# Forward attention of a decode block on one Trainium2 core: K and V of heads 32 to 111 loaded by pairs in 2 MB transfers

## The chip, the cores and the metric

The kernel runs on one core of one Trainium2 chip, in one launch. The metric is the device time of that launch in microseconds; for the kernel before the change it is the median of three runs. All data stands in HBM at the start, and all results have to be in HBM at the end.

## What is computed

The program is a decode step of one transformer block (4 sequences, one token each) with its gradients. Cut to what matters here:

```python
# x: (4, 1, 512); k_cache, v_cache: (4, 32, 4096, 128); all bfloat16
q = (layernorm(x) @ wq).reshape(4, 1, 32, 128).transpose(0, 2, 1, 3)
p = softmax(einsum("bhqd,bhkd->bhqk", q, k_cache) * 128 ** -0.5)
o = einsum("bhqk,bhkd->bhqd", p, v_cache)
h = x + o.transpose(0, 2, 1, 3).reshape(4, 1, 4096) @ wo
out = h + (silu(layernorm(h) @ w1) * (layernorm(h) @ w3)) @ w2
# returned: out, and the gradients of x, k_cache, v_cache, wq, wo, w1, w3, w2 for a given grad_out
```

4 sequences times 32 heads make 128 "heads" s, with sequence b = s % 4 and head h = s // 4. Each has 1 MB of K and 1 MB of V. The program reads K once (134 MB), V twice (268 MB) and writes the gradients of both caches (268 MB).

## The kernel before

Everything is written in one fixed order; each engine works through its own instructions in that order and waits on semaphores. There are three stretches.

**Forward** (`for gi in range(NGI)`, L653 to L715): 64 steps `gi`, two heads a step. For the two heads of a step: `T_pe` and `T_dve` transpose K (a quarter on TensorE, copied out by ScalarE in L362; three quarters on VectorE in 32x32 blocks of 32-bit words, L367). `S_head` makes the scores of both heads in one PSUM tile of 128 x 256 with 32 small matmuls (L393), whose stationary parts (`W`, `zq`) GpSimd prepares one step ahead in `q_stationaries` (L373, L375). Softmax is spread over the engines: `sm_max` (VectorE, L400 and L402), `sm_max_T` (TensorE, L407), `sm_gmax` (VectorE, L412), `sm_bcast` (TensorE, L417), `sm_exp` (VectorE copy L422, ScalarE L425), `sm_sum` (TensorE L431), `sm_norm` (VectorE L436, ScalarE L439), `sm_P` (TensorE L446, four ScalarE copies L450 into `P_all`). Then `PK_pairs` (GpSimd, L456) writes P twice beside each other, and `PK_mul` (VectorE, L460) multiplies K by P. `M_mm` (TensorE, L475) sums, over 32 groups of 128 keys, V-transposed times [P*K, P]: 32 matmuls of 128 rows x 128 columns by 130 columns into one PSUM bank. `M_end` adds P*K over the keys with ones as stationary operand (L485) and copies the sum M out (ScalarE, L489). M (kept until the gradients) holds what the gradient of q needs and the output o.

A step does the softmax of its own heads, the transposes of the next step's heads (`na`, `nb`), and `M_mm`/`M_end` of two heads that lie 3 and 2 behind (`m1`, odd; `m2`, even). `M_mm(m1)` is split into 16 and 16 matmuls around `sm_max_T`, `M_mm(m2)` into 24 and 8 around `sm_P`. Every 32 heads `kP_flush` empties the P*K sums; every 16 heads `O_cols` copies columns of o.

**Middle** (L717 to L972): output projection, layer norm, the gated MLP and its gradient; a chain of small steps.

**Backward** (L975 to L1519): V again, gradients of V (L816, L1403 on VectorE) and of K, written out 1 MB at a time for heads 0 to 31 and by pairs of heads (2 MB, 64 keys per partition for each head) for heads 32 to 127; `P_rows` (L1357) builds for these pairs the pair layout of P from `P_all`.

**Buffers and queues.** K, V, transposed K, PK, M and all weights live in `arena`, 23 slots of 1 MB (a little more, for alignment). `Slot` takes the slot that has been free longest; `give` returns it. All large transfers are issued by SyncE in program order and pass through one queue, first in, first out. Each load waits, on SyncE, for the last readers of its slot. `load_K` fills K up to 8 heads ahead (`more_K`, after each `PK_mul`), `load_V` always 3 heads ahead (`VQ`, after each `M_end`). In both, partition p of a head holds keys 32p to 32p+31, so a transfer is 128 rows of 8 KB.

Of the kernel before, what the change touches and what calls it, by code (L numbers as in the profile page):

```python
# [23 lines left out]
OLD = 9  # L24
LEAD = 64


@with_exitstack
def kernel(
# [80 lines left out]
    free = deque(range(NSLOT))  # L110
    part = {"B": False, "side_done": False}
    SIDE = ("Pp", "lnb", "wq2", "dqflat", "fin", "rows1", "rows2", "oflat", "w2a", "w2b", "gwq", "gw2", "gw13", "gwo")
# [13 lines left out]
    class Slot:  # L126
        def __init__(self, name, src=free):
            self.i = src[0]
            if part["B"] and src is free:
                lone = sorted((i for i in free if i not in part["pairs"]), key=age, reverse=True)  # L130
                self.i = lone[0] if name in SIDE or lone and age(lone[0]) >= OLD else max(free, key=age)
            src.remove(self.i)
            self.w = arena[:, self.i * SLOT:(self.i + 1) * SLOT]
            o = (self.i + 1) % 2 * LEAD
            self.t = self.w[:, o:o + SJ * Dh]

        def b(self, n=4096):
            return self.t[:, 0:n]
# [36 lines left out]

    Ks, Vs, KTs, PKs = {}, {}, {}, {}

    def load_K(s):
        if s < NH:
            Ks[s] = Slot("Kn")  # L180
            nc.sync.dma_start(out=Ks[s].heads(), in_=cache_head(A_k_cache, s))

    nvl = {"n": 0}

    def load_V(s):
        if s < NH and s >= nvl["n"]:
            nvl["n"] = s + 1
            Vs[s] = Slot("Vn")
            nc.sync.dma_start(out=Vs[s].heads(), in_=cache_head(A_v_cache, s))


    def more_K(s):
        while len(Ks) + kdone["n"] < min(NH, s + 8) and len(free) > 1:
            load_K(len(Ks) + kdone["n"])

    kdone = {"n": 0}
    more_K(0)


# [11 lines left out]
    for i in range(2):  # L211
# [3 lines left out]
        onesw.append(t)  # L215

    def ones_window(col):
        i = col % 2
        return onesw[i][:, 32 - i - col:64 - i - col]

    rowg = fcon.tile([P, 8], FP32, name="rowg")
    nc.vector.tensor_reduce(out=rowg[:], in_=ident_f.rearrange("p (c g q) -> p g c q", c=4, q=4), axis=AX.XY, op=ALU.add)
    quad = fcon.tile([P, 4], FP32, name="quad")
    nc.vector.tensor_reduce(out=quad[:], in_=ident_f.rearrange("p (q i) -> p q i", q=4), axis=AX.X, op=ALU.add)
    bsum = fcon.tile([P, P], FP32, name="bsum")
    nc.vector.tensor_copy(out=bsum.rearrange("p (c g q) -> p c g q", c=4, q=4),
                          in_=rowg[:, None, :, None].to_broadcast([P, 4, 8, 4]))
    maskneg = fcon.tile([P, G], FP32, name="maskneg")  # L230
    nc.vector.tensor_scalar(out=maskneg[:], in0=rowg[:, 0:G], scalar1=-1.0, scalar2=1e30, op0=ALU.add, op1=ALU.mult)
    wmask = fcon.tile([P, G, 32], BF16, name="wmask")
    nc.gpsimd.memset(wmask[:], 0.0)
    for g in range(G):
        nc.vector.tensor_copy(out=wmask[:, g, 4 * g:4 * g + 4], in_=quad[:])
    selg = fcon.tile([G, P], FP32, name="selg")
# [63 lines left out]
    with ExitStack() as c0:  # L300
        ps0 = c0.enter_context(tc.tile_pool(name="ps0", bufs=1, space=bass.MemoryType.PSUM))
        sg = ps0.tile([G, P], FP32, name="sg_ps")
        nc.tensor.transpose(sg[:], rowg[:, 0:G], ident_f[:])
        nc.vector.tensor_scalar(out=selg[:], in0=sg[:], scalar1=-scale, scalar2=None, op0=ALU.mult)
# [64 lines left out]
    def q_stationaries(gi):  # L369
        W = fw.tile([P, G, 4, 32], BF16, name="W", tag="W", bufs=1)  # L370
        for hl in range(G):
            s = gi * G + hl
            nc.gpsimd.tensor_tensor(out=W[:, hl], in0=qrep[:, :, s:s + 1].to_broadcast([P, 4, 32]),  # L373
                                    in1=wmask[:, hl, None, :].to_broadcast([P, 4, 32]), op=ALU.mult)
            nc.gpsimd.tensor_copy(out=zq[hl][:, 32:132:67], in_=qT_bf[:, s:s + 1].to_broadcast([P, 2]))  # L375
        hold[gi] = {"W": W}

    def S_head(gi, hl):
        s = gi * G + hl
        st = hold[gi]  # L380
        if hl == 0:
            st["S"] = psS.tile([P, JQ * 32], FP32, name="S_ps", tag="S")
        KT = KTs[s].heads()
        KT5 = KT.rearrange("p j (r l t) -> p j r l t", r=2, t=2)
        for k in range(4):
            for c in range(4):
                if c < NPE:
                    lhsT = zq_window(zq[hl], 4 * hl + k)
                    rhs = KT[:, c * JQ:(c + 1) * JQ, 32 * k:32 * (k + 1)]
                else:  # L390
                    lhsT = st["W"][:, hl, k, :]
                    rhs = KT5[:, c * JQ:(c + 1) * JQ, k // 2, :, k % 2]
                nc.tensor.matmul(st["S"][32 * c:32 * (c + 1), :], lhsT=lhsT, rhs=rhs, start=(hl == 0 and k == 0),  # L393
                                 stop=(hl == G - 1 and k == 3), tile_position=(0, 32 * c))
        KTs.pop(s).give()
# [46 lines left out]
    def sm_P(gi):  # L442
        st = hold[gi]
        pt = psT.tile([P, JQ, P], BF16, tag="tps", name="pt_P")
        for jj in range(JQ):
            nc.tensor.transpose(pt[:, jj, :], st["Pn"][:, jj].rearrange("p q l -> p (q l)"), ident_b[:])  # L446
        v = pt.rearrange("p jj (c g q) -> p g c jj q", c=4, q=4)
        for q in range(4):
            r_ = slice(32 * q, 32 * (q + 1))
            nc.scalar.copy(out=P_all[r_, gi * G:(gi + 1) * G, :].rearrange("p g (c jj) -> p g c jj", c=4),  # L450
                           in_=v[r_, 0:G, :, :, q])

# [5 lines left out]
    def PK_mul(s):  # L458
# [7 lines left out]
        Ks.pop(s).give()  # L466
        kdone["n"] += 1

    def M_mm(s, j0, j1):
        if j0 == 0:  # L470
            hold["M"] = psM.tile([P, PKW], FP32, name="M_ps", tag="M")
        PK = PKs[s].w[:].rearrange("p (j c) -> p j c", c=PKW)
        Vn = Vs[s].heads()
        for j in range(j0, j1):
            nc.tensor.matmul(hold["M"][:], lhsT=Vn[:, j, :], rhs=PK[:, j, :], start=(j == 0), stop=(j == SJ - 1))  # L475

    def M_end(s):
        w = s % 32
        PK = PKs[s].w[:].rearrange("p (j c) -> p j c", c=PKW)
        if w == 0:  # L480
            hold["kP"] = psK.tile([P, 4, Dh], FP32, name="kP_ps", tag="kP")
        for c in range(2):
            for q in range(4):
                j0 = (c * 4 + q) * 4
                nc.tensor.matmul(hold["kP"][32 * q:32 * (q + 1), :, :], lhsT=ones_window(w), rhs=PK[:, j0:j0 + 4, 0:Dh],  # L485
                                 start=(w == 0 and c == 0), stop=(w == 31 and c == 1), tile_position=(0, 32 * q))
        if s % MC == 0:
            Ms.append(Slot("M"))
        nc.scalar.copy(out=M_of(s), in_=hold["M"][:, 0:Dh + 1])  # L489
        PKs.pop(s).give()  # L490
        Vs.pop(s).give()
# [138 lines left out]

    def weights(gi):
        if gi in reserve:
            while nvl["n"] < NH and len(free) > reserve[gi]:
                load_V(nvl["n"])
            pump(reserve[gi])
# [6 lines left out]

    for s in range(VQ):
        load_V(s)
    q_stationaries(0)
# [7 lines left out]
    for gi in range(NGI):  # L653
# [6 lines left out]
        S_head(gi, 1)  # L660
        weights(gi)
        if has1:
# [14 lines left out]
        if has1:  # L677
            M_end(m1)
            load_V(m1 + VQ)
            if m1 % 32 == 31:  # L680
# [14 lines left out]
        if hasp:  # L695
            PK_mul(pk1)
            more_K(pk1 + 1)
        weights(gi)
        if has2:
            M_mm(m2, 0, 24)  # L700
        sm_P(gi)
        if has2:
            M_mm(m2, 24, SJ)
            M_end(m2)
            load_V(m2 + VQ)
        weights(gi)
        PK_pairs(a)
        if nxt:
            T_dve(nb, 2, 2)
        PK_mul(a)  # L710
        more_K(a + 1)
        weights(gi)
        hold.pop(gi - 3, None)
        if 2 <= gi:
            step("d")  # L715

    c1b.close()  # L717
    c1b = ExitStack()
# [256 lines left out]
    with ExitStack() as c2:  # L975
# [310 lines left out]

        def two(t):
            s = SP + t // B * 2 * B + t % B
            return s, s + B

        def two_heads(ap, t):
            b, h = t % B, H0 + t // B * 2
            return ap[b, h:h + 2].rearrange("h (p j) d -> (h p) (j d)", p=P // 2)

# [58 lines left out]

        def P_two(t, n=2):
            return Pp["s"].b(NT * 2 * SJ).rearrange("p (t j) -> p t j", j=2 * SJ)[:, t:t + n, :]

        def P_rows(q):  # L1357
            if q >= NT // B or q in Pp:
                return
            if not Pp:  # L1360
# [8 lines left out]
                P2b.extend(x[:, n + i * 4 * SJ:n + (i + 1) * 4 * SJ].rearrange("p (j t) -> p j t", t=2) for i in range(2))  # L1369
            Pp[q] = True  # L1370
            ps = psrep.tile([P, B, 2, SJ], FP32, tag="rep", name="Pp_ps")
            s = SP + q * 2 * B
# [177 lines left out]
```

## Time and profile before

| | |
|---|---|
| median of 3 runs | 1686.53 us (1684.51 to 1686.71) |
| the profiled execution | 1683.1 us, of which the span from first to last instruction is 1681.3 us |
| busy time over the span | PE 1259.9 us (75%), DVE 1233.6 us (73%), ACT 961.0 us (57%), POOL 380.8 us (23%) |
| moved | 707.21 MB in 80987 packets, mean 421 GB/s; queue 1 busy 99.4% of 16 engines' span |
| forward, V times PK (L475) | 4096 matmuls, 286.0 us, mean 222 ns |
| forward, P times K (L460) | 128 instructions, 292.5 us, mean 2285 ns |
| issues of the forward caches | 128 of 1 MB for K (14.8 us to landing), 128 of 1 MB for V (among 160 V loads of 1 MB, 15.3 us to landing) |
| granted TensorE clock | 0.853 over the span, 0.98 to 1.00 from 40 to 655 us |

The profile is one execution, taken by the hardware profiler. PE is TensorE's matmuls, PEld its weight loads (beside the matmuls), DVE VectorE, ACT ScalarE, POOL GpSimd, SP SyncE. "L475" is line 475 of the kernel. A matmul's recorded 222 ns is its way through the array; one can start 0.06 us after the other, so that a sum of these durations says nothing of how densely they follow each other. Idle time of an engine stands with what ended it.

### The profile page before, as it was taken

The page shows a single profiled execution, that of the slowest core. Times are in us where ns is not written, and L with a number is a line of the kernel's source. Part 1 is how long each engine was busy: PE and PEld are TensorE (multiplying, and loading weights), DVE is VectorE, ACT ScalarE, POOL GpSimd, SP SyncE. Part 2 cuts the span into 40 slices and gives each one's busy share as a digit, 9 for nine tenths or more (in the row PEclk, how much of TensorE's full clock was granted, in tenths as well). Part 3 has the DMA queues.
Part 4 walks back from the last instruction along what each step waited for, and adds up shares of the span by engine and source line. Part 5 has one row for each costly group of instructions (what it writes and reads, how often), then busy time and mean ns, then how long its engine had stood idle before and what let it go on. Part 6 is the DMA issues. An engine that isn't in the chain of part 4 may idle for free.

```text
span 1681.3 us, 33967 instructions
## 1 busy us (share of the span) xinstructions
PE 1259.9 (75%) x14188; PEld 919.9 (55%) x14188; DVE 1233.6 (73%) x1198; ACT 961.0 (57%) x1492; POOL 380.8 (23%) x663
## 2 busy tenths in 40 slices
PE   5889888888888888878887766667766777777660
PEld 4677776677677666645555544534444444444430
DVE  5989899989998997667767476576565656555673
ACT  3455454445544454676666656666665676666650
POOL 2211222322232222235540131121220101010120
PEclk8999999999999999998889878787678676666675
DMA  9999999999999999999999999999999999999996
GB/s 400 425 425 424 425 424 425 425 425 423 418 425 410 424 414 403 411 411 425 426 426 428 429 430 430 430 429 431 429 429 431 428 430 429 431 429 430 431 430 277
DMA packets 80987, 707.21 MB, mean 421 GB/s; under 512 B 8749, under 2 KB 12985, under 8 KB 15297
## 3 DMA queue, kind: packets, MB, share of 16 engines
q1 hardware_dynamic: 80416, 704.94, 99.4%
q8 instruction: 112, 1.84, 0.4%
q14 instruction: 43, 0.34, 0.0%
q0 software_dynamic: 416, 0.10, 0.0%
HBM read 422.59 MB, written 282.34 MB: 419 GB/s over the span
## 4 chain that ended last, share of the span: by engine, by line
DMA 36%; DVE 8%; ACT 4%; PE 4%; issue 3%; DVEq 0%; SPq 0%; POOL 0%; ACTq 0%
DMA out_dram<-arena 35%; DVE arena L1403 7%; ACT arena L802 4%; PE pt_tps L801 1%; PE dq_ps L1010 1%; DMA arena<-in_A_v_cache_dram 1%; PE dP_ps L1248 1%; PE pt_wo L613 0%; DVE arena L816 0%; DVEq L1545 0%; PE rep_ps L1189 0%; DVE dPr L1345 0%; PE dOT_ps L776 0%; ACT dPr L1224 0%; PE dPT_ps L1231 0%
## 5 line engine op out<-in xcount | busy, mean ns | idle before, releaser
L802 ACT COPY arena<-pt_tps 128x1024 bf16<-128x1024 bf16 x512 | 492.0, 1022 | 243.9 <-PE pt_tps L801 240.5
L801 PE MATMUL pt_tps<-ident_f,arena 128*128 128x128 f32 x2048 | 410.3, 355 | 198.4 <-DMA arena<-in_A_v_cache_dram 122.2
L801 PEld LDWEIGHTS pt_tps<-ident_f,arena 128*128 128x128 f32 x2048 | 302.9, 181 | 345.1 <-issue 188.4
L1403 DVE TENSOR_TENSOR arena<-arena 128x8192 bf16<-128x8192 bf16 x48 | 212.5, 4427 | 191.9 <-DMA out_dram<-arena 187.9
L460 DVE TENSOR_TENSOR arena<-arena 128x4096 bf16<-128x4096 bf16 x128 | 292.5, 2285 | 22.8 <-POOL arena L456 21.7
L475 PE MATMUL M_ps<-arena 128*128 128x130 bf16 x4096 | 286.0, 222 | 13.1 <-DMA arena<-in_A_v_cache_dram 12.9
L475 PEld LDWEIGHTS <-arena 128*128 128x128 bf16 x4096 | 254.9, 100 | 31.2 <-DMA arena<-in_A_v_cache_dram 20.0
L1403 DVE TENSOR_TENSOR arena<-dS,arena 128x8192 bf16<-128x8192 bf16 x48 | 212.3, 4424 | 68.6 <-DMA out_dram<-arena 68.6
L367 DVE STREAM_TRANSPOSE arena<-arena 128x512 f32<-128x512 f32 (+1 forms) x321 | 250.6, 797 | 0.0
L362 ACT COPY arena<-pt_tps 128x1024 bf16<-128x1024 bf16 x128 | 129.4, 1012 | 169.9 <-PE pt_tps L361 137.9
L1400 POOL COPY arena<-arena 128x128 bf16<-128x128 bf16 x48 | 45.3, 945 | 426.1 <-ACT arena L1377 197.9
L373 POOL TENSOR_TENSOR W<-qrep,wmask 128x128 bf16<-128x128 bf16 x128 | 120.9, 945 | 85.5 <-PE S_ps L393 70.8
L456 POOL COPY arena<-P_all 128x64 bf16<-128x64 bf16 x128 | 32.7, 255 | 411.1 <-ACT P_all L450 408.1
L1311 POOL COPY arena<-arena 64x4 bf16<-64x4 bf16 x96 | 64.5, 672 | 141.4 <-PE dP_ps L1331 114.1
L1331 PE MATMUL dP_ps<-arena 128*32 128x512 bf16 x768 | 85.1, 482 | 7.0 <-ACT arena L802 6.7
L816 DVE TENSOR_TENSOR arena<-dS,arena 128x4096 bf16<-128x4096 bf16 x32 | 73.1, 2290 | 20.2 <-DMA out_dram<-arena 20.0
L425 ACT ACTIVATE E<-S_ps,nm 128x256 f32<-128x256 f32 x64 | 30.4, 475 | 92.9 <-DVE nm L422 92.8
L450 ACT COPY P_all<-pt_P 32x64 bf16<-32x64 bf16 x256 | 52.1, 203 | 52.6 <-PE pt_P L446 50.3
L361 PE MATMUL pt_tps<-ident_b,arena 128*128 128x128 bf16 x1024 | 80.7, 223 | 0.0
L485 PE MATMUL kP_ps<-arena,onesw 128*32 128x512 bf16 x1024 | 79.6, 388 | 0.0
L816 DVE TENSOR_TENSOR arena<-P,arena 128x4096 bf16<-128x4096 bf16 x29 | 66.3, 2291 | 17.6 <-DMA out_dram<-arena 16.9
L994 PE MATMUL gps<-arena 4*128 4x512 bf16 x110 | 46.0, 441 | 40.8 <-ACT arena L988 40.8
(246 smaller groups left out, 1495.3 us busy)
## 6 DMA issues: line engine op xcount, KB each, us to landing
out_dram<-arena SPq DMA_DIRECT2D x96, 2048.0 KB, 27.4
arena<-in_A_v_cache_dram SPq DMA_DIRECT2D x160, 1024.0 KB, 15.3
arena<-in_A_k_cache_dram SPq DMA_DIRECT2D x128, 1024.0 KB, 14.8
arena<-in_A_v_cache_dram SPq DMA_DIRECT2D x48, 2048.0 KB, 31.6
out_dram<-arena SPq DMA_DIRECT2D x72, 1024.0 KB, 18.4
arena<-in_A_wq_dram SPq DMA_DIRECT2D x8, 1024.0 KB, 14.3
arena<-in_B_w_dram SPq DMA_DIRECT2D x8, 896.0 KB, 15.5
out_dram<-arena SPq DMA_DIRECT2D x6, 896.0 KB, 27.8
```

The source lines that it names most:

```text
L361: nc.tensor.transpose(pt[:, i, :], Kn[:, c * GW + i, :], ident_b[:])
L362: nc.scalar.copy(out=KT[:, c * GW:(c + 1) * GW, :], in_=pt[:])
L367: nc.vector.transpose(out=KT[:, c * w_:(c + n) * w_], in_=Kn[:, c * w_:(c + n) * w_])
L373: nc.gpsimd.tensor_tensor(out=W[:, hl], in0=qrep[:, :, s:s + 1].to_broadcast([P, 4, 32]), in1=wmask[:, hl, None, :].to_broadcast([P, 4, 32 ...
L460: nc.vector.tensor_tensor(out=PK[:, :, 0:Dh].rearrange("p j (r t) -> p j r t", t=2), in0=Ks[s].heads().rearrange("p j (r t) -> p j r t", t=2),
L475: nc.tensor.matmul(hold["M"][:], lhsT=Vn[:, j, :], rhs=PK[:, j, :], start=(j == 0), stop=(j == SJ - 1))
L485: nc.tensor.matmul(hold["kP"][32 * q:32 * (q + 1), :, :], lhsT=ones_window(w), rhs=PK[:, j0:j0 + 4, 0:Dh], start=(w == 0 and c == 0), stop ...
L801: nc.tensor.transpose(ptw[:, jj, :], w[:, 4 * g + jj, :], ident_f[:])
L802: nc.scalar.copy(out=v.rearrange("p (j d) -> p j d", d=Dh)[:, g * GW:(g + 1) * GW, :], in_=pt[:])
L816: nc.vector.tensor_tensor(out=dst.rearrange("p j (r t) -> p j r t", t=2), in0=col2[:, :, None, :].to_broadcast([P, SJ, Dh // 2, 2]), in1=r ...
L1331: nc.tensor.matmul(rows["acc"][32 * c:32 * (c + 1), :], lhsT=zt[t % B][:, k, ZP - m:ZP - m + 32], rhs=words_of(v, 2 * c + u, k), start=(pl ...
L1403: nc.vector.tensor_tensor(out=dst.rearrange("p (j r t) -> p j r t", r=Dh // 2, t=2), in0=col2[:, :, None, :].to_broadcast([P, 2 * SJ, Dh / ...
```

## The change

Heads 32 to 111 (`UP = SP + 2 * NPF` = 112) are taken in 40 pairs (s, s + 4), two heads of one sequence that lie next to each other in HBM. One transfer brings K of both heads, 2 MB, 128 rows of 16 KB: partitions 0 to 63 hold head s with 64 keys each, partitions 64 to 127 head s + 4. The two 1 MB halves of such a block ("units") take the place of the two heads of a step `gi`: each unit holds half of the keys of both heads. So the number of instructions of transposes, scores, softmax and P*K is what it was, and only masks and row orders differ. `M_mm` has to keep the two heads apart: each of its 32 matmuls becomes two of 64 array rows, (0, 0) and (64, 0), into two PSUM banks, which both units of a pair add up; `M_end` copies both banks out after the second unit. `q_stationaries` makes `W` with two instructions of 64 partitions and twice the elements instead of two of 128 partitions.

All loads up to head 111 are taken two slots at a time (`Twin`: two neighbouring free slots, given back when both halves are done), those of heads 0 to 31 as two 1 MB transfers. The order of loads is one list: K of two heads, then V of two heads that lie four behind; `more`, called at five places of a step, issues from it as long as a reserve of free slots is left. `Slot` in the forward stretch takes a slot whose neighbour is in use, so that neighbouring pairs stay free. In the backward stretch `P_rows` has nothing left to do for the first 40 pairs, as `P_all` is in pair layout already.

```diff
+RES = (1, 2, 1, 1, 1)
+NPF = 40
...
+            if part["F"]:
+                self.i = next((i for i in src if i ^ 1 not in src), src[-1])
...
+    def two_heads(ap, t):
+        b, h = t % B, SP // B + t // B * 2
+        return ap[b, h:h + 2].rearrange("h (p j) d -> (h p) (j d)", p=P // 2)
...
+    def load_units(of, name, ap, n):
+        if n >= UP:
+            of[n] = Unit(name)
+            nc.sync.dma_start(out=of[n].heads(), in_=cache_head(ap, n))
+            return
+        tw = Twin()
+        of[n], of[n + 1] = Unit(name, tw, 0), Unit(name, tw, 1)
+        if pair_unit(n):
+            nc.sync.dma_start(out=tw.t, in_=two_heads(ap, (n - SP) // 2))
+        else:
+            for k in range(2):
+                nc.sync.dma_start(out=of[n + k].heads(), in_=cache_head(ap, n + k))
+    loads = deque()
+    for n in range(0, NH + 4, 2):
+        for of, name, ap, m in ((Ks, "Kn", A_k_cache, n), (Vs, "Vn", A_v_cache, n - 4)):
+            if 0 <= m < UP:
+                loads.append((of, name, ap, m))
...
+    def more(reserve):
+        while loads:
+            wide = loads[0][3] < UP
+            if len(free) < reserve + 1 + wide or wide and not Twin.choices():
+                break
+            load_units(*loads.popleft())
...
     def q_stationaries(gi):
+        if pair_unit(gi * G):
+            for a, s in enumerate(pair_heads((gi * G - SP) // 2)):
+                r_ = slice(64 * a, 64 * (a + 1))
+                nc.gpsimd.tensor_tensor(out=W[r_], in0=qrep[r_, None, :, s:s + 1].to_broadcast([64, G, 4, 32]),
+                                        in1=wmask[1][r_, :, None, :].to_broadcast([64, G, 4, 32]), op=ALU.mult)
+                nc.gpsimd.tensor_copy(out=zq[a][:, 32:132:67], in_=qT_bf[:, s:s + 1].to_broadcast([P, 2]))
...
     def M_mm(s, j0, j1):
-        if j0 == 0:
-            hold["M"] = psM.tile([P, PKW], FP32, name="M_ps", tag="M")
+        pr = pair_unit(s)
+        if j0 == 0 and not (pr and s % 2):
+            hold["M"] = [psM.tile([P, PKW], FP32, name="M_ps", tag="M") for _ in range(1 + pr)]
...
         for j in range(j0, j1):
-            nc.tensor.matmul(hold["M"][:], lhsT=Vn[:, j, :], rhs=PK[:, j, :], start=(j == 0), stop=(j == SJ - 1))
+            if pr:
+                for a in range(2):
+                    r_ = slice(64 * a, 64 * (a + 1))
+                    nc.tensor.matmul(hold["M"][a][:], lhsT=Vn[r_, j, :], rhs=PK[r_, j, :], start=(s % 2 == 0 and j == 0),
+                                     stop=(s % 2 == 1 and j == SJ - 1), tile_position=(64 * a, 0))
+            else:
+                nc.tensor.matmul(hold["M"][0][:], lhsT=Vn[:, j, :], rhs=PK[:, j, :], start=(j == 0), stop=(j == SJ - 1))
...
     def M_end(s):
...
-        nc.scalar.copy(out=M_of(s), in_=hold["M"][:, 0:Dh + 1])
+        if not pair_unit(s) or s % 2:
+            for M, h in zip(hold["M"], hs):
...
+                nc.scalar.copy(out=M_of(h), in_=M[:, 0:Dh + 1])
...
+        more(reserve.get(gi, RES[k] + (2, 3, 4)[gi] if gi < 3 else RES[k] + (gi % 8 in (1, 2))))
...
         def P_two(t, n=2):
+            if t < NPF:
+                return P_all[:, SP + 2 * t:SP + 2 * (t + n), :].rearrange("p (t h) j -> p t (h j)", h=2)
...
+            if q < NPF // B:
+                return
             ps = psrep.tile([P, B, 2, SJ], FP32, tag="rep", name="Pp_ps")
```

Left out of the diff: the masks and sums for the two row orders (`row_of`, `cls`, `bsum`, `wmask`), which are built once at the start, and `ones_window2`, the stationary operand of L485 for a pair.

## The prediction

> **What bounds the kernel now.** First the page, for the queues and the DMA share:
>
> ```profile
> q1 hardware_dynamic: 80416, 704.94, 99.4%
> q8 instruction: 112, 1.84, 0.4%
> ```
>
> The transfers fill the span, so one reads: DMA-bound, and a faster transfer is a gain. The stages tell more. By windows of 32 heads (columns: PE, PEld, DVE, ACT, POOL busy, clock, DMA share, GB/s):
>
> ```profile
> 206.90:366.60 159.70, 136.48 (x2265) 112.12 (x2264) 148.51 (x197) 78.82 (x178) 43.12 (x97) 0.99 1.01 425
> 366.60:526.20 159.60, 137.18 (x2265) 112.26 (x2264) 148.52 (x198) 78.83 (x178) 42.78 (x97) 0.99 1.01 421
> ```
>
> DVE is busy for 93%, DMA all the time. Which one sets the pace? Between starts of L400 (one a step) lie 9.73 to 9.80 us in step after step; only `O_cols` (10.6) and `kP_flush` (12.6) lengthen it. Such evenness is a chain's, not a queue's. One step of the timeline:
>
> ```profile
> 206.91 0.42 DVE L400 TENSOR_REDUCE mx<-S_ps 128x1 f32<-128x256 f32 x1
> ...
> 207.34 0.40 POOL L373 TENSOR_TENSOR W<-qrep,wmask 128x128 bf16<-128x128 bf16 x1
> 207.36 0.41 DVE L402 TENSOR_SCALAR mxm<-maskneg,mx 128x2 f32<-128x2 f32 x1
> ...
> 207.82 0.27 PE L407 MATMUL x_ps<-ident_f,mxm 128*2 128x128 f32 x1 [0.89 <-DVE mxm L402]
> ...
> 207.93 1.10 PE L475 MATMUL M_ps<-arena 128*128 128x130 bf16 x16
> ...
> 208.96 0.38 PE L417 MATMUL b_ps<-gm,selg 2*128 2x1 f32 x2
> ...
> 209.37 0.16 DVE L422 COPY nm<-b_ps 128x1 f32<-128x1 f32 x1 [0.21 <-PE b_ps L417]
> ...
> 212.59 0.62 PE L446 MATMUL pt_P<-ident_b,Pn 128*128 128x128 bf16 x8 [0.54 <-ACT Pn L439]
> ...
> 214.44 2.29 DVE L460 TENSOR_TENSOR arena<-arena 128x4096 bf16<-128x4096 bf16 x1 [0.27 <-POOL arena L456]
> ```
>
> DVE waits twice a step, 0.21 us for nm and 0.27 us for P; its 9.27 us of work and these two make 9.75. The first wait stands behind 16 matmuls of `M_mm(m1)`: L417 starts when they end. So the forward is a DVE chain with PE in it, and DMA keeps just up: bytes issued and not yet landed (issue times against packet ends, over 425 GB/s) are worth 9 to 13 us at 240 to 360, 3 to 7 at 600 to 640, and 0.8 at least near 700. DMA runs empty there. A step that gets longer therefore moves the end almost one for one; a shorter one moves it at most as far as DMA got faster.
>
> Early the queue does bind:
>
> ```profile
> PEld L475 <- DMA arena<-in_A_v_cache_dram: 8.4, 10, 1.9
> ```
>
> (waits from 20 to 206 us.) Three steps there take 11.02, 11.81 and 10.10 us for 9.74: 3.7 us lost to late V.
>
> **The transfers.** A packet of 8 KB takes 309 ns, one of 16 KB 611 (medians of the packet records, the latter in the backward stretch), the record that ends a transfer 9. Per engine, 2 MB cost 16 x 309 + 2 x 9 = 4962 ns now and 8 x 611 + 9 = 4897 after: 65 ns x 80 = 5.2 us; with means (311.4, 612.4), 7.4. Against it, 2560 more matmuls with as many weight loads: the page's 1.84 MB on q8 for 28376 PE instructions are 65 bytes each, so 0.33 MB more, 20 packets of 930 ns over 16 engines, 1.2 us. Net -4.0 to -6.2 us of DMA work, off the path while the chain sets the pace: it is the floor of any gain.
>
> **The order of loads.** Counting the loads in program order at 2.48 us each against the steps that use them, V is 2 to 3 us late from head 6 on now, since K is asked for 2 steps ahead and V 1.4. In the new list nothing is late up to head 31: -3.7 us. But a pair is usable only when all 2 MB are there: K of heads 32 to 35 comes 2 us late by the same count: +2.0. A pair of slots is free when the later of its two readers is done, and all further loads stand behind that wait on SP. Still, later leads are 2.1 to 2.6 steps, 1.1 at heads 96 to 111 (11 us for 2 MB of 4.9): no wait. Sum -1.7.
>
> **V times PK.** Twice the matmuls, each half as deep. Neighbouring matmuls of L475 start 0.059 us apart. If the halves overlap, a pair takes that; if not, 0.118. No matmul of 64 rows is in the trace. The nearest rows: 32 columns wide (L393), four start within 0.107 us where one streams 256 columns, so parts of the array do work side by side, an instruction each 13 ns, and a pair's four in 0.059 us is no denser. I take 0.060, by L393; the bounds are 0.059 and 0.118. 16 pairs ahead of L417: +0.02 us a step.
>
> Passing between shapes costs: L475 to L485 (32 columns) starts 0.150 after, against 0.059 to L361 (same shape): 0.091. L475 to L417 (2 rows) is 0.150 already. New passages: L407 to L475 (on the path, +0.09), L475 to L361 (inside the 0.89 us that PE waits for mxm), L431 to L475 and L475 to L446 (inside the 0.54 for Pn), L446 to L475. [...]
>
> Both copies of M now stand behind `sm_exp` on ACT (0.26 us, 0.17 apart). Behind them waits L362, which PE's transposes hold until 0.38 after the first copy starts: nothing added (7 us if PE came earlier). `M_mm(m2)` now waits for both banks; behind it on PE stands L446, for which ScalarE's L450, POOL and in the end L460 wait. It is 0.1 to 0.2 later, inside the 0.54; without that cover, 4 to 8 us. In the three `O_cols` and two flush steps the second copy is on the path: +0.8.
>
> **GpSimd.** L402 needs 0.23 us alone (steps 0, 8, 14, 63) but 0.41 in 59 steps: it ends 0.02 after the second W of L373. After the change W is twice as long per instruction: the first, held back by L460, ends about 0.61 instead of 0.35 us after L400 starts, so L402 waits for that and gets in ahead of the second: ends near 0.71 instead of 0.86, -0.15. If the second got in first: +0.45. I take the first, as in steps 0, 8, 14, where L402 came between the two.
>
> Together per step: -0.15 + 0.09 + 0.02, -0.04 x 40 = -1.6. [...]
>
> **Slots for PK.** Followed through program order, 23 of the 40 steps give `PK_pairs(a)` the slot that `M_end(m2)` has just released, so that L456 waits for L485 of m2, and behind it the next W on POOL and L460 on DVE; now it is 7. Those steps (from 49) take 9.79 for 9.745: 0.045. With the passage L446 to L475 and slower halves, 0.15: 23 x 0.15 - 7 x 0.045 = +3.1.
>
> Set-up adds some 3 us of small DVE work ahead of 7.3 us that DVE waits for the first q: hidden (3 us if not). Less `P_rows` (40 matmuls, 10 copies of 0.37) lies where DMA binds: nothing.
>
> Sum: -1.7 - 1.6 + 0.8 + 3.1 = +0.6 us; 1683.1 becomes 1683.7. The median stands 3.4 above the profiled execution: 1687.1.
>
> **Rivals.** *The halves don't overlap* (slower). 0.118 a pair: +0.94 ahead of L417, and 24 pairs overrun the 0.54 us by 0.95: +1.9 a step, 76 us. PE's own work, 8.5 us busy in a step of 9.75, plus 3.8 plus 0.45 of passages, makes 12.7: +118. So 1763 to 1804. It decides from 0.08 a pair, where the 0.54 us is used up; a pace of 0.075 to 0.1 costs 10 to 35. [...] Against it: L393.
>
> *The chain gets shorter* (faster). L402 gains the 0.18 that it loses now, the passage costs nothing, the K of 32 is in time: -3.7 - 0.15 x 40 and more, and DMA's floor cuts it at -4 to -6.2: 1680.3 to 1682.5. For it: early V waits are in the trace. Against: the PK slots.
>
> *W holds L402 longer* (slower): +0.45 instead of -0.15, 0.6 x 40 = 24 us: 1711. Against: steps 0, 8, 14.
>
> That 16 KB rows don't become 16 KB packets is excluded: the backward stretch shows them for the same access.
>
> **Numbers.** Forecast (overlap, chain within 0.2 us a step) 0.50, its own range 1682 to 1695; shorter chain 0.20; W 0.10; intermediate pace 0.10 (1697 to 1722); full serial 0.10. A measurement here tells 0.2% (3.4 us) from no change. Faster: 0.20 and 0.05 of the forecast. Same: 0.30. Slower: 0.15 of the forecast and the rest, 0.45. Range 1680.5 to 1716 leaves out the serial case and some of the rest.
>
> **What would show it.** After: L475 of 64 rows starting two within 0.06 us; L402 near 0.26 long; nm's wait near 0.3; steps of 9.7 in the 30s and 9.85 where PK waits for L485; no V waits before 200; K late once at about 170; q1's packets down by 11500 (144 per pair and cache); DMA emptier near 700. Wrong if L475 pairs start 0.08 or more apart, or L402 takes 0.8.

## The result, and the profile after

| | before | after |
|---|---|---|
| median | 1685.17 us (1683.77 to 1686.71, 7 runs) | 1698.55 us (1693.71 to 1705.94, 7 runs) |
| ratio after / before | | 1.008, 95% interval 1.0059 to 1.0101 |
| the profiled execution | 1683.1 us, span 1681.3 | 1693.71 us, span 1691.9 |
| start of the last step's L400, now L495 | 654.25 us | 663.75 us |
| from there to the end | 1027.1 us | 1028.2 us |

The change costs 13 us, and single runs spread over 12 us where they spread over 3 before. Of the 10.6 us between the two spans, 9.5 arise in the forward stretch. First the queues of the page after:

```profile
q1 hardware_dynamic: 68896, 704.93, 98.9%
q8 instruction: 131, 2.15, 0.5%
```

Data packets are 11520 fewer, as counted, and instruction packets 19 more, where 20 were counted. But the data queue is no longer full all the time, and the windows (columns as before: PE, PEld, DVE, ACT, POOL busy, clock, DMA share, GB/s) say where:

```profile
206.90:366.60 159.70, 139.37 (x3166) 108.69 (x3167) 142.13 (x190) 74.90 (x175) 45.01 (x90) 0.99 1.01 425
366.60:526.20 159.60, 137.98 (x3210) 107.99 (x3206) 141.10 (x189) 73.28 (x173) 50.36 (x95) 1.00 0.98 401
```

421 GB/s became 401 from 366 to 526 us, at the same clock, while DVE is busy for 141 us instead of 149. The other engines are not at their limit either (GpSimd 50 of 160 us, 43 before; TensorE 138, 137 before), and the data queue has room: something waits. A step that goes well looks as forecast (timeline; the last bracket is the idle time before and its cause):

```profile
460.00 0.41 DVE L495 TENSOR_REDUCE mx<-S_ps 128x1 f32<-128x256 f32 x1
...
460.45 0.23 DVE L497 TENSOR_SCALAR mxm<-cw,mx 128x2 f32<-128x2 f32 x1
...
460.81 0.62 POOL L461 TENSOR_TENSOR W<-qrep,wmask 64x256 bf16<-64x256 bf16 x1
...
460.94 1.11 PE L574 MATMUL M_ps<-arena 64*128 64x130 bf16 x32
...
462.39 0.16 DVE L517 COPY nm<-b_ps 128x1 f32<-128x1 f32 x1 [0.32 <-PE b_ps L512]
```

L497 (L402 before) takes 0.23 instead of 0.41 us, ahead of the second `W`. 32 matmuls of 64 rows (L574) take 1.11 us, as long as the 16 of 128 rows before (1.10): the halves overlap. The next L495 stands at 469.65, a step of 9.65 us. That next step is another matter:

```profile
469.65 0.42 DVE L495 TENSOR_REDUCE mx<-S_ps 128x1 f32<-128x256 f32 x1
...
470.81 0.45 PE L574 MATMUL M_ps<-arena 64*128 64x130 bf16 x9 [1.71 <-issue]
...
471.64 0.27 PE L502 MATMUL x_ps<-ident_f,mxm 128*2 128x128 f32 x1
```

In the middle of a row of V-times-PK matmuls, with operands and banks at hand, TensorE does nothing for 1.7 us; "issue" is the profile's word for a wait without a visible cause. L502, which stands 0.74 us behind L495 in the good step, comes 1.99 behind it here, and the step takes 10.93 us. From 206 to 640 us the waits (total, times, longest) read

```profile
PEld L574 <- issue: 26.1, 67, 1.9
DVE nm L517 <- PE b_ps L512: 18.4, 43, 1.2
PE M_ps L574 <- issue: 12.6, 17, 1.7
PE S_ps L488 <- issue: 6.3, 4, 1.7
```

Before the change the same two rows of code (L475 and L393) have issue waits of weight loads alone, none of matmuls:

```profile
PEld L475 <- issue: 6.4, 28, 0.2
PEld L393 <- issue: 0.5, 3, 0.2
```

What comes in at such a moment? This gap lasts from 469.10 to 470.81. A look at the DMA packets of one microsecond around its start, 468.4 to 469.4 (packets, MB, share of 16 engines):

```profile
q1 hardware_dynamic: 22, 0.31, 98.8%
q8 instruction: 1, 0.02, 5.9%
```

One instruction packet of 16384 bytes: by the packet records it moves from 468.43 to 469.38, and TensorE goes on at 470.81. So it is everywhere. From 100 to 640 us TensorE pauses 17 times for over 0.35 us (neither a matmul nor a load runs) with "issue" as the cause, 18.0 us in all; before the change it never does. Each of these pauses ends 1.19 to 1.49 us after an instruction packet has landed (median 1.39), and after it the next instruction packet begins to move 3.84 us later (median). Hence theory A: TensorE has used up its instructions and waits for the next packet. At the 65 bytes that the prediction found for one instruction, 16384 bytes would hold some 252, an estimate; the records of TensorE give the number. Count all records of TensorE (matmuls, loads, semaphore instructions) ahead of the first one after a pause: at all 17 it is 193 + 256 x k, where k is the number of instruction packets that have landed by then (no run shows what the 193 are). So one packet stands for 256 records, every pause stands at the same place among these 256, by theory A the end of a packet, and lasts until 1.19 to 1.49 us after the next one has landed. 49 packets in the 45 steps from 200 to 640 us made some 280 instructions a step; the 128 that a pair step adds make some 410. So a packet lasted 9.0 us (median distance of packets) and now lasts 6.2. From the step into one packet to the use of the next pass, at these pauses, 3.84 us until it moves, 0.94 to move and 1.4 until it can be used: 6.2 us. There is nothing to spare.

### The profile page after: what moved, and what is told of

Its sections match the earlier page's. It is cut to its first block, busy times and chain, and to the rows that moved or that the text cites. A ratio compares the mean times of both kernels' runs of the same rounds, so it can differ in the third digit from the quotient of the medians.

```text
span 1691.9 us, 38716 instructions
## 1 busy us (share of the span) xinstructions
PE 1266.8 (75%) x16708; PEld 914.6 (54%) x16708; DVE 1230.3 (73%) x1218; ACT 951.6 (56%) x1482; POOL 418.1 (25%) x670
## 5 line engine op out<-in xcount | busy, mean ns | idle before, releaser
L901 PE MATMUL pt_tps<-ident_f,arena 128*128 128x128 f32 x2048 | 404.7, 351 | 214.3 <-DMA arena<-in_A_v_cache_dram 135.2
L901 PEld LDWEIGHTS pt_tps<-ident_f,arena 128*128 128x128 f32 x2048 | 298.5, 179 | 356.3 <-issue 199.6
L556 DVE TENSOR_TENSOR arena<-arena 128x4096 bf16<-128x4096 bf16 x128 | 292.4, 2284 | 22.5 <-POOL arena L552 22.1
L574 PE MATMUL M_ps<-arena 64*128 64x130 bf16 x5120 | 182.7, 218 | 13.8 <-issue 12.6
L574 PEld LDWEIGHTS <-arena 64*128 64x128 bf16 x5120 | 151.1, 95 | 36.1 <-issue 26.3
L1405 POOL COPY arena<-arena 64x4 bf16<-64x4 bf16 x96 | 102.3, 1065 | 210.6 <-PE dP_ps L1425 182.3
L552 POOL COPY arena<-P_all 128x64 bf16<-128x64 bf16 x128 | 31.0, 242 | 389.6 <-ACT P_all L546 357.3
L577 PE MATMUL M_ps<-arena 128*128 128x130 bf16 x1536 | 106.8, 222 | 0.0
L461 POOL TENSOR_TENSOR W<-qrep,wmask 64x256 bf16<-64x256 bf16 x80 | 93.1, 1164 | 50.6 <-PE S_ps L488 47.4
L577 PEld LDWEIGHTS <-arena 128*128 128x128 bf16 x1536 | 95.9, 100 | 6.2 <-issue 5.9
L1498 POOL COPY arena<-P_all 128x128 bf16<-128x128 bf16 x40 | 25.4, 635 | 246.3 <-DVE arena L1501 245.3
L916 DVE TENSOR_TENSOR arena<-P,arena 128x4096 bf16<-128x4096 bf16 x29 | 66.1, 2287 | 17.7 <-DMA out_dram<-arena 16.4
L448 PEld LDWEIGHTS <-arena 128*128 128x128 bf16 x1024 | 60.3, 100 | 34.3 <-PE b_ps L512 15.4
```

The source lines that it names most:

```text
L448: nc.tensor.transpose(pt[:, i, :], Kn[:, c * GW + i, :], ident_b[:])
L461: nc.gpsimd.tensor_tensor(out=W[r_], in0=qrep[r_, None, :, s:s + 1].to_broadcast([64, G, 4, 32]), in1=wmask[1][r_, :, None, :].to_broadcas ...
L556: nc.vector.tensor_tensor(out=PK[:, :, 0:Dh].rearrange("p j (r t) -> p j r t", t=2), in0=Ks[s].heads().rearrange("p j (r t) -> p j r t", t=2),
L574: nc.tensor.matmul(hold["M"][a][:], lhsT=Vn[r_, j, :], rhs=PK[r_, j, :], start=(s % 2 == 0 and j == 0), stop=(s % 2 == 1 and j == SJ - 1), ...
L577: nc.tensor.matmul(hold["M"][0][:], lhsT=Vn[:, j, :], rhs=PK[:, j, :], start=(j == 0), stop=(j == SJ - 1))
L901: nc.tensor.transpose(ptw[:, jj, :], w[:, 4 * g + jj, :], ident_f[:])
```

## Experiments

Rivals were that the larger data packets hold the instruction packets back (B), that the order of loads and the twin slots cost the time (C), and that the passages between shapes (0.091 us by the prediction's reading of before) and the two banks do (D). The expectations call these passages drains; the trace shows how long they take, not what the array does in them. In the first four runs parts are taken out or stand alone. Medians of before on the chips used were 1685.4 (first four runs), 1685.1 (next four) and 1684.9 (last three).

**No pairs, the new order of loads.**

```diff
-NPF = 40
+NPF = 0
```

> The new kernel with no pairs (NPF = 0): the new list of loads, twins of slots for heads 0 to 31 and the new set-up stay; all heads are single, with 128-row matmuls. Theory A (TensorE runs out of instructions: its 16 KB instruction packets come too late for bursts of V-times-PK matmuls that are used up twice as fast): no idle time of TensorE that ends 1.2 to 1.6 us after an instruction packet has landed, the early V waits gone, so 1681 to 1685 us against 1685 before. Rival B (16 KB data packets hold the instruction packets back): the same 1681 to 1685, as these are gone too. Rival C (the order of loads and the twin slots cost the time): 1688 to 1698, since the list and the twins are still there.

1685.94 us, ratio 1.0004 (0.9995 to 1.0013): no matmul has an issue wait from 206 to 640 us. C falls for the list of loads; twins are left for heads 0 to 31 alone here, so the rest of C has to wait for the next run. The last step starts at 651.45 us, 2.8 earlier than before the change, but the end gains nothing.

**Matmuls of 128 rows.**

```diff
-                for a in range(2):
-                    r_ = slice(64 * a, 64 * (a + 1))
-                    nc.tensor.matmul(hold["M"][a][:], lhsT=Vn[r_, j, :], rhs=PK[r_, j, :], ...
+                nc.tensor.matmul(hold["M"][0][:], lhsT=Vn[:, j, :], rhs=PK[:, j, :], ...
...
```

> The new kernel with each pair of 64-row matmuls replaced by one of 128 rows into one bank, copied out twice: the sums of the two heads of a pair are not kept apart. Loads of 2 MB, twins, order, W by halves and both copies stay. Theory A: the instructions of TensorE are as many as before the change, no idle time behind instruction packets, steps of 9.55 to 9.75 us, 1676 to 1684. Rival B (16 KB data packets): idle time stays, at least half of it, 1688 to 1695. Rival C (loads and slots): 1693 to 1699, as after the change. Rival D (not the supply but the drains between shapes and the dependence on two banks): 1680 to 1686, and no irregular idle time in either.

1682.34 us, 0.9981 (0.9972 to 0.9989). With all else of the change in place, the time falls below that of before. Its waits from 206 to 640 us:

```profile
PEld L572 <- DMA arena<-in_A_v_cache_dram: 17.0, 23, 1.4
DVE nm L517 <- PE b_ps L512: 10.4, 44, 0.3
PEld L572 <- issue: 8.9, 39, 0.2
```

No issue wait of these matmuls is over 0.2 us, and good steps take 9.61. All twins and 2 MB loads are there, so C falls altogether. TensorE waits for V instead: the chain has become faster than the transfers.

**Two transfers of 1 MB for a pair.**

```diff
-            nc.sync.dma_start(out=tw.t, in_=two_heads(ap, (n - SP) // 2))
+            for k in range(2):
+                h_ = slice(k * SJ * Dh, (k + 1) * SJ * Dh)
+                nc.sync.dma_start(out=tw.t[:, h_], in_=two_heads(ap, (n - SP) // 2)[:, h_])
```

> The new kernel with the load of a pair issued as two transfers of 1 MB, 8 KB a row each, into the same twin: layout, matmuls, order and slots as after the change, data packets of 8 KB as before it. Theory A: the idle time of TensorE stays, 1694 to 1703 us (the 1698.6 of the change, and up to 5 more of DMA work that is mostly hidden). Rival B: the 8 KB packets let instruction packets through, idle time behind them gone, 1683 to 1690. Rival C: as after the change.

1692.93 us, 1.0044 (1.0032 to 1.0057): just under what A gave, above what B gave. The pauses stay with 8 KB packets (15 in place of 17, 19 in the repeat below), so B is no main cause. The next instruction packet moves 3.71 us after a pause instead of 3.84 (3.88 in the repeat): a small part of it may be B.

**The 64-row matmuls alone,** in the kernel before the change, for heads 32 to 111.

```diff
-            nc.tensor.matmul(hold["M"][:], lhsT=Vn[:, j, :], rhs=PK[:, j, :], ...
+                for h_ in range(2):
+                    r_ = slice(64 * h_, 64 * (h_ + 1))
+                    nc.tensor.matmul(hold["M"][h_][:], lhsT=Vn[r_, j, :], rhs=PK[r_, j, :], ...
...
```

> The kernel before the change with its loads, order and slots, but for heads 32 to 111 each V-times-PK matmul in two of 64 array rows into two banks, summed over an even and an odd head and copied out after the odd one (the sums mix heads: timing only). Theory A: idle time of TensorE that ends 1.2 to 1.6 us after an instruction packet, some 20 us of it between 200 and 640 us, half of that on the path: +8 to +14 us, 1693 to 1699. Rival B (needs 16 KB data packets): no such idle time, 1685 to 1690 by the drains alone. Rival C: 1685 to 1687.

1697.10 us, 1.0064 (1.0052 to 1.0077): nearly the whole loss, without one changed transfer. Waits from 206 to 640 us:

```profile
PEld L479 <- issue: 18.2, 60, 1.1
PE M_ps L479 <- issue: 6.4, 11, 1.0
PE S_ps L393 <- issue: 4.5, 3, 1.8
```

Good steps take 9.84 us instead of 9.74, since `W` is as before here. The passage from L407 to the first V-times-PK matmul, on the path, takes 0.203 us here and 0.108 before the change, as much as that 0.1: some 4 us of the 8.7 that the steps 18 to 56 got longer. The rest lies in single steps, and all 12 pauses (10.4 us) again end at the place among the 256 where, by theory A, a packet begins. So D has a share here, and the pauses, some of them beside other work, the rest.

**Alternate halves,** which parts the number of instructions from the shapes: even groups of keys in the upper rows, odd ones in the lower.

```diff
-                for a in range(2):
+                for a in (j % 2,):
...
```

> The new kernel, but each of the 32 groups of keys of a unit is summed in one half only: even groups with array rows 0 to 63 into the first bank, odd ones with rows 64 to 127 into the second (half of the keys are left out). TensorE's instructions are as many as before the change; 64-row shapes, passages between shapes, both banks, 2 MB loads and twins stay. Theory A (supply: 256 instructions of one packet must not be used up in less than some 6 us): no idle time that ends 1.2 to 1.6 us after an instruction packet, steps of 9.6 to 9.75, 1681 to 1686 us. Rival D (drains between shapes, two banks, neighbouring row tiles): the time stays above 1690, with steps longer evenly.

1682.22 us, 0.9981 (0.9972 to 0.9990). Shapes, passages, banks, slots and transfers are those of the change, the number of instructions is that of before, and the loss is gone. There is no pause any more: the matmuls have no issue wait at all, their loads short ones; the wait is for data:

```profile
PEld L574 <- DMA arena<-in_A_v_cache_dram: 40.8, 32, 2.7
PEld L574 <- issue: 12.0, 52, 0.4
```

Good steps are 9.2 us here (half of the work), others 10 to 11.7, and the last step starts at 650.83, as in the run with 128 rows (650.71): that is what the transfers allow. So D does not make the loss by itself: its 0.1 us a step, if still there, is hidden behind the transfers.

**Half of V.** Does the instruction packet come late because the queue is full?

```diff
+        if pair_unit(n) and of is Vs:
+            of[n + 1] = Unit(name, tw, 0)
+            nc.sync.dma_start(out=tw.t[:, 0:SJ * Dh], in_=two_heads(ap, (n - SP) // 2)[:, 0:SJ * Dh])
```

> The new kernel, but for V of heads 32 to 111 only the first 8 KB of each 16 KB row is loaded, and both units use it (half of V is left out): 40 MB less in the forward stretch, so the data queue runs empty there, and TensorE's instructions are as many as after the change. Theory A in the form that an instruction packet is late because it waits among data packets: with the queue empty at times, the idle time behind instruction packets falls to a third or less of the 24 us, steps near 9.7, the last step starts near 656 us instead of 664; the whole is shorter by that and by what 40 MB less (up to 95 us of queue time) give the DMA-bound middle. If the packet takes its 6 us whatever else is moved, the idle time stays near 24 us and the last step starts at 662 to 665.

1685.87 us, 1.0002 (0.9993 to 1.0011). The last step starts at 655.79, as expected; but the idle time was to fall to a third or less, and it fell only to about half (8 pauses, 8.6 us, for 17 and 18.0):

```profile
PEld L577 <- issue: 19.6, 53, 1.8
PE M_ps L577 <- issue: 8.0, 7, 1.6
```

The queue was thinner, not empty:

```profile
206.00:366.00 160.00, 142.90 (x3305) 113.08 (x3299) 146.13 (x197) 76.43 (x178) 52.41 (x98) 0.99 0.84 321
```

Where little was left on it, the next packet came sooner. After four of the 8 pauses all data issued so far landed within 3.2 to 4.6 us, and the next instruction packet moved 1.32 to 2.85 us later; after the other four the data took 5.0 to 10.5 us and the packet 3.7 to 4.2. All other profiles agree: where the data issued so far took 5.0 us or more, the packet took 3.5 to 5.5, and the one time it took less (3.9, in the change itself) the packet took 1.93. So part of the wait, an estimated 1 to 2.5 of the 3.8 us by these figures, is spent behind data. The missing 40 MB did not shorten the rest: from the last step to the end still 1030 us, so this stretch does not hang on what is saved before it. That part of the expectation was wrong.

**The change again, and 16 pairs.** The first repeats the change, on the chip of the last two runs. The second has `NPF = 16` and makes `W` of single heads as that of pairs:

```diff
-            nc.gpsimd.tensor_tensor(out=W[:, hl], in0=qrep[:, :, s:s + 1].to_broadcast([P, 4, 32]), ...
+            r_ = slice(64 * hl, 64 * (hl + 1))
+            nc.gpsimd.tensor_tensor(out=W[r_], in0=qrep[r_, :, s:s + G].rearrange("p k g -> p g k")[:, :, :, None] ...
```

> The kernel after the change, on the same chip as the others of this call: 1696 to 1700 us, 1.006 to 1.010 of before; the spread of single runs some 4 to 12 us, since each stall depends on when a packet comes through.

> The new kernel with 16 pairs only (heads 32 to 63), and W of all single heads made as in the pairs, by two instructions of 64 partitions and both heads. Theory A with the figures so far: order of loads -2.6 us and 0.13 us a step from W over 48 steps, -6, for the forward; 16 pairs x 0.24 us of stalls, +4; DMA work 16 x 0.13 = -2 us. The forward ends some 5 us earlier than before the change, and the end follows as far as the DMA work got shorter: 1682.5 to 1685, against 1685.4. Rival (any pair costs through slots and loads, not instructions): 1687 to 1691.

The change: 1695.41 us (1691.65 to 1699.03), 1.0061 (1.0048 to 1.0074), a little under the expected time, with the same waits (PE L574 11.5 us, 17 times; 19 pauses, 16.4 us). 16 pairs: 1684.02, 0.9994 (0.9985 to 1.0003): as expected, and 11 us better than the change, a gain over before that the interval doesn't separate from none. Single steps take 9.55 us with the new `W`; the forward ends 2.4 us earlier than before the change (last step at 651.87), where 5 were expected.

**A few instructions fewer.** If the supply is short by so little, a small cut must help much.

```diff
-        for c in range(2):
+        for c in range(0 if pair_unit(s) and 0 < s % 32 < 31 else 2):
```

> The new kernel with the P-times-K sums over the keys left out in all pair units but the first and the last of each 32: 16 TensorE instructions fewer in each of 75 units, 30 in a step of some 412. V-times-PK, loads, slots and copies as after the change. Theory A: 256 instructions last 9.74 x 256 / 382 = 6.5 us instead of 6.05, and a packet needs 5.9 to 6.2 us from the step into the packet before it until it can be used; so a small cut of 7% of the instructions should take away more than half of the idle time and of the loss: 1684 to 1689 us. Rival D (drains, banks): fewer passages as well, 2 x 0.09 us a step off PE's path, mostly hidden: 1692 to 1696.

1686.31 us, 1.0007 (0.9998 to 1.0016), last step at 654.70: 7% fewer TensorE instructions take away 9 to 12 of the 10 to 13 us. The median distance of the instruction packets is 6.53 us, and the waits are half (8 pauses, 8.1 us):

```profile
PEld L574 <- issue: 16.9, 52, 1.5
PE M_ps L574 <- issue: 6.2, 7, 1.4
PEld L574 <- DMA arena<-in_A_v_cache_dram: 9.8, 15, 2.0
```

The cut also takes away two passages and 1.2 us of matmuls a step, which run beside other work.

**No pairs with the new W, and 24 pairs.** `NPF = 0` and `NPF = 24` in the kernel with 16 pairs.

> No pairs (NPF = 0), the new list of loads, and W of all heads by two instructions of 64 partitions and both heads: the chain gets some 0.18 us a step shorter, 9.55 us as in the single steps of e8. If the transfers then set the end, as e1 says (the forward 2.6 us shorter, the end the same), it gives 1684.5 to 1686.0, no better than before. If the chain were still the bound: 1675 to 1680.

> As e8, but 24 pairs (heads 32 to 79) instead of 16: another 1 us of DMA work less; 8 more pair steps of about 10.1 us for 9.55, 4 us more in the forward. If the transfers still set the end: 1682.5 to 1683.5; if the forward does by then: 1684.5 to 1688.

Without pairs 1686.28 us, 1.0006 (0.9997 to 1.0014), just above the 1686.0 expected where the transfers set the end: steps of 9.56 us, yet the last one starts at 651.58, as without the new `W` (651.45), because TensorE now waits for V:

```profile
PEld L578 <- DMA arena<-in_A_v_cache_dram: 23.5, 28, 2.2
```

24 pairs: 1686.84, 1.0012 (1.0003 to 1.0022), last step at 655.97, with 14 pauses: the forward sets the end. With 1 MB transfers a faster chain runs into the transfers; with more pairs the instructions eat what the transfers give. Of the versions that compute the whole, 16 pairs came out lowest, but not clear of before.

## Why the prediction was right in part and wrong in its sum

The forecast was no change (1687.1 us); the measured 1698.55 lies inside the range, in the part that "slower" (0.45) had been given for other reasons. That is luck: neither the sum nor a rival has the wait that made the loss, and of the two signs of being wrong (pairs of L475 0.08 apart, L402 0.8 long) none came. By its steps:

- **What bounds the kernel: right.** Longer steps moved the end nearly one for one (9.5 us in the forward, 10.6 in the span); shorter ones gained nothing without faster transfers (no pairs: 2.8 us earlier, end unchanged).
- **Transfers, gain: right in kind, too large in size.** The two runs that reach the floor (128 rows, alternate halves) came out 3.0 and 2.8 us below before, and they have no more instructions than before, so that the prediction's own figure for them is -5.2 to -7.4. Part of the difference stands in the packets: 16 KB took 611 ns in the median, as assumed, but 618 and 617 in the mean from 206 to 640 us, and 628.7 in the change itself, where the sum took 612.4 from the backward stretch. At 628.7, 2 MB cost 5039 ns per engine, no less than the 5007 of 8 KB packets (311.8 in the mean) before.
- **Transfers, instructions: the step that failed.** The 2560 matmuls were turned into 20 packets (19 came) and priced at their share of queue time, 1.2 us. Here bytes are not what they cost. A packet stood for 256 instructions and took 6.2 us from one pause to the use of the next; from 256 in 6.0 to 6.2 us I estimate that TensorE got no more than 41 to 43 instructions per us beside the full data queue, and the change asks for 410 in 9.74 us, 42. The sum has no term for that wait. The steps 18 to 56 take 389.7 us; 375.8 with matmuls of 128 rows. These 13.9 us hold the gaps and at most 0.1 us of passages a step; so the gaps are 10 or more.
- **Order of loads.** V waits are gone as said: none stands in the list up to 206 us; at the start of the ninth step the change is ahead by 1.7 us and in its repeat by 3.5 (forecast 3.7). Late K of heads 32 to 35 made the sixteenth and seventeenth step together 0.5 us longer in one execution and 2.7 in the other (forecast 2.0).
- **Halves overlap: right.** 32 matmuls in 1.11 us; the rival of 0.118 a pair falls, although a load of 64 rows takes 95 ns in the mean where one of 128 rows took 100. **Passages: right.** From L502 to L574 0.203 us, 0.108 from L407 to L475 before: 0.095, forecast 0.09 on the path.
- **GpSimd: right.** L497 ends 0.68 us after L495 starts, forecast 0.71. The rival in which `W` holds it longer falls. Good steps take 9.65 to 9.74, forecast 9.70.
- **Slots for PK: the wait came, its price didn't.** From 206 to 640 us L552 on GpSimd waits for V-times-PK matmuls 15 times, 11.0 us (5.6 with 128 rows), where 23 of 40 steps were forecast; but L556 on VectorE, which the +3.1 us were to reach, waits for L552 hardly longer than before (22.1 us over the whole kernel, 21.7 before).
- **The intermediate pace** (1697 to 1722) had the right time, but by slower halves, which did not come.

From the landing of the packet before the one that ends a pause to the start of the pause, TensorE has 256 to 384 records, at all 17: it had little in hand there. The longest pause took 1.75 us. The four gaps of S_ps (L488) have the same cause: they are among the 17 pauses and stand at the same place of the 256 like the rest.

What stays open: which part of the 6 us is fixed and which hangs on the queue; whether instructions alone do it, since no run adds instructions without adding matmuls; why single runs of the change spread so much (it fits packets that come by chance early or late in a burst of matmuls, but was not traced run by run), and how much of the loss a smaller data packet would save.

## What to carry to other kernels

Count instructions on an engine as a supply, not as bytes: where the data queue is full, compare how many instructions the busiest engine uses per us with what a packet of 16 KB brings (256 here) and with the distance at which such packets come (9.0 us here before the change, 6.2 after). The split of a matmul in two that overlap cost no time in the array here (32 in 1.11 us for 16 in 1.10), and it doubled the instructions. In the profile look for "issue" waits in the midst of matmuls that need nothing, for instruction packets that land just before they end (here 1.19 to 1.49 us), and for a whole number of packets' instructions between them (here multiples of 256); then take instructions away before anything else. And before shortening a chain that already runs beside a full queue, see what the queue allows: here 0.18 us less in each of 64 steps moved nothing.

## What the runs showed of the hardware

- TensorE stood still for up to 1.8 us with "issue" as the cause. In the eight profiles with pairs of 64-row matmuls (after, its repeat, two 1 MB transfers, halves alone, half of V, 16 and 24 pairs, fewer sums) there are 100 such pauses from 100 to 640 us, and all 100 stand at the same place of a packet's 256 instructions, by theory A its end; in the other five profiles there is none.
- Work resumed 1.37 to 1.48 us (median of each run) after the 16 KB packet had landed. The next packet began to move 3.5 to 5.5 us after that where the data issued so far took 5.0 us or more to land (95 times), 1.3 to 2.9 us where it took less (5 times).
- Few instructions decided: at some 410 a step of 9.74 us the loss was 10 to 13 us in 40 steps (the change and its repeat), at some 380 it was 1.5 (fewer sums; by its interval 0 to 3).
- Two matmuls of 64 rows in the two halves of the array took together what one of 128 rows took (32 in 1.11 us against 16 in 1.10).
- One `W` instruction of 64 partitions and twice the elements in place of one of 128 let VectorE's small L497 through: 0.23 us instead of 0.41, good steps of 9.55 us where single heads use it.
